# A tuned attention-plus-FFN kernel: broadcasting the reciprocal denominators in 16 reads with the head outermost in DRAM, and an instruction order that counts the issue time of transfers

## The chip, the cores and the metric

One core of one Trainium2 chip runs the whole kernel. The metric is the device time of one execution in microseconds (us). Executions of one kernel mostly agree within 0.5%. In what follows PE is TensorE (the matmuls), ACT is ScalarE, DVE is VectorE, POOL is GpSimd, and "the queue" is SyncE's, which issues every transfer.

The instructions of every engine are laid out in advance: the program holds a small scheduler that plans each operation with a counted duration and then emits one fixed list per engine. So a count in that plan that is wrong does not slow anything by itself; it puts instructions into an order that does not fit the chip.

## The reference, cut to what matters

Shapes: S = 2048 tokens, D = 1024, 32 heads of 32, F = 3584, bf16.

```python
xn = layernorm(x)
qkv = (xn @ wqkv) ...                                  # 32 heads of 32
pq, pk = phi(q), phi(k)                                # phi = elu + 1 + 1e-6
kv  = einsum("bhsd,bhse->bhde", pk, v);  z = sum_s pk
num = einsum("bhqd,bhde->bhqe", pq, kv)
den = einsum("bhqd,bhd->bhq", pq, z) + 1e-6            # one number per head and token
s = (num / den) @ wo
ffn = (silu(xn @ w_gate) * (xn @ w_up)) @ w_down
out = x + s * silu(ffn)
```

The kernel computes 1/den on a few partitions ("rows" below: one row per head), writes it to DRAM, and reads it back broadcast, each head's row to the 32 partitions that hold this head's 32 features. It then multiplies phi(q) by it before the projection.

## The kernel before: the parts that matter

The plan: an operation with a semaphore is a transfer. `free[e]` is when its queue can issue the next, `o.done` when it has landed.

```python
o.start = s
if o.sem is not None:
    free[e] = s + 0.08
    dma_free = max(s, dma_free) + o.nbytes / 310e3
    o.done = max(s + o.nbytes / 190e3, dma_free) + 1.2
else:
    ...
    free[e] = s + o.busy
    o.done = s + o.busy + o.lat
```

The denominators: for each half of the heads eight writes of 8 KB after the reciprocals, then `normalise`, which fills one tile of rows `RB` (128 partitions x 1024 elements, 256 KB) with four reads, scales it on ACT, and multiplies on DVE. It runs eight times, so there are 16 tiles, 64 reads, 32 scalings and 32 multiplies.

```python
for p in range(2):
    for q in range(4):
        t0 = (q % 2) * 256
        dma([rb], [named("rscr", p, q, s)], r_scr[p, q // 2, 16 * s:16 * s + 16, t0:t0 + 256],
            ...,  dsem("rs%d%d%d" % (p, q, s)), 8 * KB, asap=True)

def normalise(p, j, half):
    for g2 in range(2):
        RB = tmp(F2)
        rba = lambda RB=RB: vap(RB).rearrange("p (g t) -> p g t", t=512)
        for hl in range(4):
            rows = r_scr[p, j].rearrange("(g h) t -> h g t", h=4)[hl, 4 * half + 2 * g2:4 * half + 2 * g2 + 2]
            dma([...], [named("rb", RB.id, hl)], lambda ...: rba()[32 * hl:32 * hl + 32, :, :],
                rows.partition_broadcast(32), lambda ...: dsem("rr%d_%d" % (RB.slot, hl)), 64 * KB, asap=True, hold=[RB])
        for gl in range(2):
            ...
            act([z_r] + [named("rb", RB.id, hl) for hl in range(4)], [RB], zr, zr, ACT.Identity, 512, "sb", scale=zc[:, g:g + 1])
            tt([sr, RB], [sr], src.bitcast(FP16), src, zr, ALU.mult, 512, True, NE[half])     # NE = ("dve", "dve")
    ... # the product goes to q_scratch in DRAM
```

At the end the queue of transfers waits once on every semaphore that was used:

```python
for s in semn.values():
    if id(s) in PL.count:
        prog["sp"].append(("w", s, PL.count[id(s)]))
```

## Time and profile before

| what, kernel before | value | where it is from |
|---|---|---|
| time, median of 4 runs | 770.14 us (767.01 to 770.58) | timed runs |
| profiled execution | span 764.9 us, mean granted clock of TensorE 0.983 | the page |
| reads of rows | 64 of 64 KB, 2.1 us from issue to landing | the page's transfer issues |
| ACT's wait on them | 14.6 us | the waits |
| PE's waits, 150 to 260 us | 25.0 us | sum of the waits' rows |
| time in which the trace has the clock at half | 28.1 us | the trace's clock records |

### The profile page before, as it was taken

Reading aid. Unit: us, or ns where it says so; the run is one execution under the profiler, and the core shown is the slowest. Engines: PE = TensorE matmul, PEld = TensorE weight load, DVE = VectorE, ACT = ScalarE, POOL = GpSimd, SP = SyncE. Lnnn points to the kernel's source line nnn. Section 1 sums busy time; section 2 is a strip of 40 time slices with the busy share of each in tenths; the row PEclk is TensorE's granted clock in tenths of the full one; section 3 lists DMA queues with packets and bytes.
Section 4 is the critical chain, followed back from the end, with each engine's and each line's share of the span. In section 5 each row is a group of like instructions: output and inputs, shape, how many; then the busy total and the mean of one; then the engine's idle time right before and its main releaser. Section 6 shows DMA issues by size and latency. Waiting matters only on the chain.

```text
span 764.9 us, 11503 instructions
## 1 busy us (share of the span) xinstructions
PE 719.4 (94%) x4091; PEld 389.4 (51%) x4121; DVE 575.1 (75%) x1109; ACT 358.8 (47%) x677; POOL 257.8 (34%) x230
## 2 busy tenths in 40 slices
PE   8999998986969699999999999999999999999996
PEld 3444454442425366666666666665554444444442
DVE  6999766987999988888878888879997752433423
ACT  3577554866738354555555545544565111111111
POOL 2011100031592746678665687903460000000000
PEclk9999999998979899999999999999999999999999
DMA  9243314233465274313333314235599282926421
GB/s 309 76 111 70 81 26 156 71 108 114 135 181 186 87 243 129 101 56 91 102 97 104 95 52 139 69 107 180 163 359 298 78 254 83 260 91 199 131 78 40
DMA packets 142698, 101.56 MB, mean 133 GB/s; under 512 B 19504, under 2 KB 137520, under 8 KB 142640
## 3 DMA queue, kind: packets, MB, share of 16 engines
q1 hardware_dynamic: 142640, 100.82, 43.9%
q8 instruction: 32, 0.52, 0.3%
q14 instruction: 26, 0.21, 0.1%
HBM read 68.16 MB, written 29.49 MB: 128 GB/s over the span
## 4 chain that ended last, share of the span: by engine, by line
PE 77%; DVE 13%; DMA 4%; SPq 2%; issue 2%; ACT 1%; DVEq 0%; ACTq 0%
PE ps L416 77%; DVE SB L474 9%; SPq L486 2%; DMA SB<-q_scratch 1%; DMA SB<-in_A_x_dram 1%; DVE ps L474 1%; DVE SB L1032 1%; ACT SB L466 1%; DMA SB<-in_B_w_up_dram 1%; DMA SB<-r_scratch 1%; DVE SB L1030 0%; DVE stats L990 0%; DVE stats L991 0%; ACT ps L466 0%; DVE SB L1282 0%
## 5 line engine op out<-in xcount | busy, mean ns | idle before, releaser
L416 PE MATMUL ps<-SB 128*128 128x512 f16 (+3 forms) x3970 | 709.7, 339 | 34.6 <-DVE SB L474 16.4
L416 PEld LDWEIGHTS ps<-SB 128*128 128x128 f16 (+1 forms) x4000 | 383.7, 98 | 358.9 <-DVE SB L474 25.6
L474 POOL TENSOR_TENSOR SB<-SB 128x1024 f16<-128x1024 bf16 (+3 forms) x196 | 244.1, 1276 | 250.8 <-DMA SB<-in_B_w_up_dram 187.1
L466 ACT ACTIVATE SB<-ps 128x256 f32<-128x256 f32 (+4 forms) x397 | 214.4, 558 | 209.0 <-PE ps L416 195.3
L474 DVE TENSOR_TENSOR SB<-SB 128x512 f16<-128x512 f16 (+10 forms) x314 | 205.0, 687 | 71.9 <-DMA out_dram<-SB 21.0
L474 DVE TENSOR_TENSOR SB<-ps,SB 128x512 f16<-128x512 f32 (+2 forms) x318 | 182.7, 592 | 49.8 <-PE ps L416 45.3
L474 DVE TENSOR_TENSOR ps<-ps,SB 128x512 f32<-128x512 f32 (+1 forms) x238 | 123.0, 531 | 40.3 <-PE ps L416 34.6
L466 ACT ACTIVATE ps<-ps 128x512 f32<-128x512 f32 (+1 forms) x166 | 82.0, 495 | 124.4 <-PE ps L416 115.5
L466 ACT ACTIVATE SB<-SB 128x512 f16<-128x512 f32 x68 | 42.0, 619 | 48.3 <-DVE SB L474 47.4
L1032 DVE SCALAR_TENSOR_TENSOR SB<-ps,SB 128x512 bf16<-128x512 f32 x49 | 32.7, 680 | 0.3
L994 POOL TENSOR_TENSOR rstd<-veps,neg_half 128x1 f32<-128x1 f32 x16 | 11.1, 699 | 64.1 <-DVE veps L993 58.0
L1030 DVE TENSOR_SCALAR SB<-SB 128x512 f16<-128x512 f16 x64 | 18.7, 299 | 15.9 <-ACT SB L466 15.7
L466 ACT ACTIVATE SB<-SB,zc 128x512 bf16<-128x512 bf16 x32 | 22.1, 720 | 16.6 <-DMA SB<-r_scratch 14.6
L466 ACT ACTIVATE SB<-SB,nmr,rstd 128x1024 f16<-128x1024 bf16 x12 | 14.8, 1232 | 0.9 <-DVE nmr L996 0.7
L990 DVE BATCH_NORM_STATS2 stats<-SB 128x6 f32<-128x512 bf16 x16 | 10.9, 682 | 4.5 <-DMA SB<-in_A_x_dram 4.5
L1032 DVE SCALAR_TENSOR_TENSOR SB<-SB 128x512 bf16<-128x512 f32 x15 | 10.9, 727 | 0.1
L991 DVE BATCH_NORM_STATS2 stats<-SB 128x6 f32<-128x512 bf16 x16 | 10.9, 680 | 0.0
L416 PE MATMUL ps<-SB,ident 128*128 128x512 f16 x17 | 5.7, 502 | 1.4 <-POOL ident L497 1.4
L445 PE MATMUL ps<-ident,SB 128*128 128x128 f16 x40 | 3.1, 220 | 2.6 <-DVE SB L1000 1.6
L445 PEld LDWEIGHTS ps<-ident,SB 128*128 128x128 f16 x40 | 2.3, 98 | 4.4 <-DVE SB L1000 2.6
L1282 DVE RECIPROCAL SB<-SB 128x64 f32<-128x64 f32 x8 | 4.3, 539 | 0.0
L416 PEld LDWEIGHTS ps<-SB,ident 128*128 128x128 f16 x17 | 2.0, 124 | 4.2 <-issue 2.2
(28 smaller groups left out, 23.1 us busy)
## 6 DMA issues: line engine op xcount, KB each, us to landing
h_scratch<-SB SPq DMA_DIRECT2D x112, 128.0 KB, 1.7
SB<-h_scratch SPq DMA_DIRECT2D x16, 896.0 KB, 6.3
SB<-in_A_x_dram SPq DMA_DIRECT2D x32, 256.0 KB, 2.9
SB<-in_B_w_gate_dram SPq DMA_DIRECT2D x14, 512.0 KB, 4.0
SB<-in_B_w_up_dram SPq DMA_DIRECT2D x14, 512.0 KB, 5.2
SB<-in_A_wqkv_dram SPq DMA_DIRECT2D x12, 512.0 KB, 7.2
SB<-in_B_w_down_dram SPq DMA_DIRECT2D x3, 1792.0 KB, 9.2
SB<-r_scratch SPq DMA_DIRECT2D x64, 64.0 KB, 2.1
```

The lines of the kernel that those rows point to most:

```text
L416: last = h.matmul(o() if callable(o) else o, l() if callable(l) else l, r() if callable(r) else r, start=st, stop=sp, skip_group_check=True)
L445: last = h.transpose(o(), i(), ident[:, :])
L466: return op("act", reads, writes, lambda h: h.activation(ev(o), ev(i), func, **kw), n / 1200.0 + (0.055 if src == "ps" else 0.095) + (0.09 ...
L474: f = lambda h: h.tensor_tensor(ev(o), ev(a), ev(b), alu)
L486: f = lambda h: h.dma_start(ev(o), ev(i))
L990: dve([xr] + ([named("ve", 0)] if q == 1 else []), [sA], lambda h: h.bn_stats(stats[:, j, 0, :], xa[:, 0:512]), 512)
L991: dve([xr] + ([named("ve", 0)] if q == 1 else []), [sB], lambda h: h.bn_stats(stats[:, j, 1, :], xa[:, 512:1024]), 512)
L994: pool([ver, nh_r], [rsr], lambda h: h.tensor_tensor(rstd[:, j, :], veps[:, j, :], neg_half[:, :], ALU.pow), 0.56)
L1030: dve([e], [e], lambda h: h.tensor_scalar(vap(e, FP16), vap(e, FP16), 1.0, EPS_PHI, ALU.min, ALU.add), 512, 3.84, urgent=PU).port = True
L1032: dve(reads + [e], [out_r], lambda h: h.scalar_tensor_tensor(out_ap, ev(src), 0.0, vap(e, FP16), ALU.max, ALU.add), 512, urgent=PU)
L1282: dve([ea], [ra], lambda h, q=q: h.reciprocal(vap(ra, F32)[:, q * 64:q * 64 + 64], vap(ea, F32)[:, q * 64:q * 64 + 64]), 400)
```

## The change

The intent is to take 48 issues off the queue of transfers (64 reads become 16), and to tell the plan what an issue really costs. To let one read cover four heads, the scratch tensor puts the head (0 to 3 in its group) outermost.

```diff
-                free[e] = s + 0.08
+                free[e] = s + o.busy
-        r_scr = nc.dram_tensor("r_scratch", [2, 2, 32, 512], BF16)
+        r_scr = nc.dram_tensor("r_scratch", [2, 2, 4, 8, 512], BF16)
-        for k in range(F2.n):
-            for hl in range(4):
-                dsem("rr%d_%d" % (k, hl))
-            return op("sp", reads, writes, f, 0.08, sem=s, nbytes=nbytes, **kw)
+            return op("sp", reads, writes, f, 1.25 if tr else 0.45, sem=s, nbytes=nbytes, **kw)
-                    Zh[:, g, 16 + 4 * (g % 4):20 + 4 * (g % 4)], hmask[:, :], ...
+                    Zh[:, g, 16 + g % 4:32:4], hmask[:, :], ...
-   (write) r_scr[p, q // 2, 16 * s:16 * s + 16, t0:t0 + 256]
+   (write) r_scr[p, q // 2, :, 4 * s:4 * s + 4, t0:t0 + 256]
-   (four reads of 64 KB, partition_broadcast(32), a semaphore each)
+                rows = r_scr[p, j, :, 4 * half + 2 * g2:4 * half + 2 * g2 + 2]
+                dma([...], [RB], partial(vap, RB),
+                    bass.AP(tensor=rows.tensor, offset=rows.offset, ap=[[4096, 4], [0, 32], [1, 1024]]), vsem(RB), 256 * KB, asap=True)
-                    act([z_r] + [named("rb", RB.id, hl) for hl in range(4)], [RB], ...
+                    act([z_r, RB], [RB], ...
```

The new source pattern has three dimensions: 4 heads, 32 copies (step 0), 1024 elements.

More of the change, by code (lines that the diff above doesn't have):

```diff
@@ L1201, in kv_end @@
                 dve([hm_r, z_r, zh_r], [named("Zh", g)], lambda h, g=g: h.tensor_scalar(
-                    Zh[:, g, 16 + 4 * (g % 4):20 + 4 * (g % 4)], hmask[:, :], zc[:, g:g + 1], None, ALU.mult), 60)
+                    Zh[:, g, 16 + g % 4:32:4], hmask[:, :], zc[:, g:g + 1], None, ALU.mult), 60)
             for c in range(2):
@@ L1287, in den_run @@
                     t0 = (q % 2) * 256
-                    dma([rb], [named("rscr", p, q, s)], r_scr[p, q // 2, 16 * s:16 * s + 16, t0:t0 + 256],
+                    dma([rb], [named("rscr", p, q, s)], r_scr[p, q // 2, :, 4 * s:4 * s + 4, t0:t0 + 256],
                         lambda p=p, q=q: vap(rb)[32 * q + 16 * p:32 * q + 16 * p + 16, 0:256],
@@ L1294, in normalise @@
                 RB = tmp(F2)
-                rba = lambda RB=RB: vap(RB).rearrange("p (g t) -> p g t", t=512)
-                for hl in range(4):
-                    rows = r_scr[p, j].rearrange("(g h) t -> h g t", h=4)[hl, 4 * half + 2 * g2:4 * half + 2 * g2 + 2]
-                    dma([named("rscr", p, 2 * j, half), named("rscr", p, 2 * j + 1, half)], [named("rb", RB.id, hl)],
-                        lambda hl=hl, rba=rba: rba()[32 * hl:32 * hl + 32, :, :], rows.partition_broadcast(32),
-                        lambda hl=hl, RB=RB: dsem("rr%d_%d" % (RB.slot, hl)), 64 * KB, asap=True, hold=[RB])
+                rows = r_scr[p, j, :, 4 * half + 2 * g2:4 * half + 2 * g2 + 2]
+                dma([named("rscr", p, 2 * j, half), named("rscr", p, 2 * j + 1, half)], [RB], partial(vap, RB),
+                    bass.AP(tensor=rows.tensor, offset=rows.offset, ap=[[4096, 4], [0, 32], [1, 1024]]), vsem(RB), 256 * KB,
+                    asap=True)
                 for gl in range(2):
@@ L1304, in normalise @@
                     zr = lambda RB=RB, gl=gl: vap(RB)[:, gl * 512:gl * 512 + 512]
-                    act([z_r] + [named("rb", RB.id, hl) for hl in range(4)], [RB], zr, zr, ACT.Identity, 512, "sb", scale=zc[:, g:g + 1])
+                    act([z_r, RB], [RB], zr, zr, ACT.Identity, 512, "sb", scale=zc[:, g:g + 1])
                     tt([sr, RB], [sr], src.bitcast(FP16), src, zr, ALU.mult, 512, True, NE[half])
```

## The prediction

> **What bounds the kernel now.** I read the page first: its slices and shares, then PE's idle time stretch by stretch, then who made PE wait there, then the chain of waits through that stretch.
>
> ```profile
> PE 719.4 (94%) x4091; PEld 389.4 (51%) x4121; DVE 575.1 (75%) x1109; ACT 358.8 (47%) x677; POOL 257.8 (34%) x230
> ```
> TensorE is busy for 719.4 of 764.9 us, so all its idle time is 45 us. Where it lies, by stretch (columns: stretch, length, then busy us and count of PE, weight loads, DVE, ACT, POOL, then granted clock, DMA share, GB/s):
>
> ```profile
> 160.00:180.00 20.00, 14.88 (x92) 6.99 (x84) 14.54 (x29) 9.32 (x19) 6.43 (x5) 1.00 0.26 74
> 180.00:200.00 20.00, 15.22 (x97) 7.36 (x98) 17.73 (x41) 15.37 (x29) 2.13 (x3) 0.83 0.50 150
> 200.00:220.00 20.00, 15.20 (x76) 7.22 (x73) 19.13 (x26) 10.32 (x19) 19.55 (x14) 0.83 0.53 150
> 220.00:240.00 20.00, 16.41 (x97) 9.89 (x97) 18.62 (x35) 12.07 (x24) 13.32 (x11) 0.91 0.39 129
> 240.00:260.00 20.00, 13.19 (x77) 7.73 (x75) 19.41 (x29) 8.62 (x17) 12.14 (x8) 0.85 0.52 173
> 260.00:290.00 30.00, 29.91 (x190) 18.50 (x189) 24.60 (x46) 15.55 (x31) 15.32 (x13) 0.98 0.60 187
> 290.00:425.00 135.00, 135.00 (x872) 84.91 (x871) 111.31 (x201) 68.92 (x142) 90.43 (x70) 1.00 0.31 93
> ```
> From 260 us on PE is full, so whatever PE gains before 260 us should reach the end undiminished. Between 160 and 260 us PE is busy 74.9 of 100 us, and the clock falls to 0.83 to 0.91 in four of the five rows: 20 x (0.17 + 0.17 + 0.09 + 0.15) = 11.6 us of clock on top of 25.1 us of idling. That is the stage in which the denominators are written, read back 64 times and applied, so the change acts where the losses are. What PE waits for there, and what ACT waits for:
>
> ```profile
> PE ps L416 <- DVE SB L474: 15.2, 6, 6.8
> PE ps L416 <- ACT ps L466: 4.8, 4, 2.0
> PE ps L416 <- ACT SB L466: 2.4, 1, 2.4
> ...
> ACT SB L466 <- DMA SB<-r_scratch: 14.6, 11, 2.7
> ```
> ACT stands 14.6 us for the broadcast rows, and because it works in order the PSUM copies behind such a wait come late: 4.8 + 2.4 = 7.2 us of PE's waits are on ACT. The larger part, 15.2 us, is on DVE. The queue of transfers in the first burst:
>
> ```profile
> 166.31 3.57 SPq L486 DMA_DIRECT2D r_scratch<-SB  x8
> 170.00 9.66 SPq L486 DMA_DIRECT2D SB<-r_scratch  x20
> 185.82 0.34 SPq L486 DMA_DIRECT2D q_scratch<-SB  x1
> 186.21 5.96 SPq L486 DMA_DIRECT2D SB<-r_scratch  x12
> ```
> One issue takes 9.66 / 20 = 0.48 us of the queue, where the kernel's own ordering counted 0.08. So the fourth tile of rows, the 16th issue, was planned about 16 x 0.4 + 8 x 0.4 = 9.6 us too early. The chain of waits goes through just these issues: SP 15.1% and the r_scratch transfers 5.0% of the 97 us from 165 to 262, that is 14.6 and 4.9 us.
>
> **What the Trainium skill says.** (1) "DMA: Bandwidth & Descriptors", section "Rules for kernel authors": coalesce many small transfers; under 64 KB they are mostly overhead. The trace agrees: 64 KB of rows land in 2.0 us, 256 KB of A_x in 2.9 us.
> (2) The same page, section "Why a DMA increments its semaphore by 16 and not by 1": a transfer runs on the largest k up to 16 that divides the slowest dimension of both access patterns. The old read has 32 rows on both sides, so k = 16. The new source is [4 heads][32 copies][1024 elements] against 128 partitions: k = 4. No row of this trace has a source like that, so it is untested here.
> (3) "GPSIMD Engine Reference", section "Specifications": GpSimd's SBUF interfaces are shared with VectorE, with contention when a DVE instruction has two SBUF inputs. The trace agrees: the 128x512 multiply that applies the rows takes 417 ns (x6, 236 to 247 us, POOL idle), 1347 ns (x6, 207 to 222 us) and 2201 ns (x4, 247 to 257 us), the last two beside a stream of POOL instructions.
> (4) "TensorE: Matmul & The Clock Gate", "What's actually happening": after an idle window the clock halves. It agrees: around 188 to 193 us 512-column matmuls average 559 ns, against 339 ns for the main group over the whole span.
>
> **The change part by part.**
> Issues: 48 fewer reads, 48 x 0.48 = 23 us less of the queue. Only the part in the chain counts, at most the 14.6 us above, and its 8 writes (3.6 us) stay: 11 us at most.
> Landing of a tile of rows: before, four issues plus 2.0 us, and the next tile 1.9 us later; the four came at about 173.4, 175.4, 177.4, 179.3 us (ACT's starts). With k = 16, 256 KB land like an A_x tile: one issue at 170.0, landing at 172.9, the others 0.5 to 0.7 us apart, the fourth at 175, 4 us earlier. With k = 4 each of four engines carries 32 packets of 2 KB. The trace's 2 KB packets take 84 ns (median), so 32 x 0.084 = 2.7 us per tile: first at 170.0 + 0.4 + 2.7 + about 1.8 = 174.9, then every 2.7 us, the fourth at 183.0 us, 3.7 us later than now. The bytes (4 MB) are the same; packets fall from 4096 to 2048.
> Queue order: plain transfers now count as 0.45, transposes as 1.25 (the trace: 0.43 to 0.48 and 1.25), so ACT and DVE are ordered to need the rows nearer to when they come. It errs the other way where k = 4, since it counts 0.85 us per tile and not 2.7. All queues are rearranged, also where nothing was wrong; I put that scatter at some 5 us either way, by judgement.
> Weight loads: the load of the next gate tile at 193.7 us follows the second q_scratch store in its buffer. Where the multiplies finish earlier, POOL's stream of 33 us from 200.3 us starts earlier too, out of its idle time before.
> The end: the queue finishes by waiting once on every semaphore, two to an instruction, 61 ns apart in the records, from 760.1 to 764.4 us, beginning right after the last store is issued. 36 semaphores of the old reads go, about one comes: 17 x 0.061 = 1.1 us less. This one is nearly sure.
> Zh with a stride of 4 in its columns, and the 8 KB writes with 4 x 4 rows: the same number of tiny operations, nothing that shows.
>
> Sum: of the 7.2 us of PE's waits on ACT I expect about 2.5 back with k = 4, and 4.5 with k = 16; of DVE's 15.2 us, 0 to 3; the clock gives 0.5 to 1.5; the end 1.1. That is about 4.5 us with k = 4 and 9 us with k = 16. I hold k = 4 for likely, at 0.7: 0.7 x 4.5 + 0.3 x 9 = 5.9 us. 770.27 - 5.9 = 764.3; I write 764.0.
>
> **The rivals.**
> The narrow transfer takes the place of the queue: engines 0 to 3 become the bound, 16 x 2.7 = 43 us of work, spread over 170 to 240 us, and large loads queue behind them. For it: the source's outer 4. Against it: only if the rows are what DVE and PE wait for. It would make 766 to 775.
> DVE is the bound anyway: it is busy 89.4 of the 100 us, 14 of them in multiplies slowed by POOL (22 at 1059 ns in 200 to 260 us against 417: 22 x 0.64 = 14 us). Rows that all land at 208 to 225 us meet POOL's stream at its densest; those of 230 to 247 us had it to themselves. Then the gain is the tail alone, about 768.
> The order comes right: ACT no longer stands, the long pauses of 2.4 to 6.8 us vanish and with them the half clock. Up to 25.1 + 11.6 us are there to win; half of it gives 752.
>
> **Range and chances.** From the full-recovery rival to the narrow-transfer one: 753 to 771. Faster by over 2% needs 15.4 us, most of PE's idling of that stage: 0.10. Slower by over 2% needs damage in stages where PE is full: 0.02. Within 2%: 0.88.
>
> **What would show it.** Right: 16 reads of 256 KB, about 7.5 us of issue in all; the semaphore sweep shorter by 1 us; ACT's wait on r_scratch below 14.6 us but not gone; 75 to 80 us of PE in the same 100; PE full afterwards. The median landing tells k: about 3 us for 16 engines, 5 us or more for 4. Wrong: PE idle in a stage that was full before (the new order did harm), multiplies still 1 to 2 us beside POOL with PE's DVE waits at 15 us or more (no gain but the tail), or the same stage at full clock with PE above 85 (far more gain than I give).

## The result

The changed kernel takes 777.76 us (median of 4, 776.7 to 778.8) beside 770.14 us: ratio 1.0108, 95% interval 1.0078 to 1.0138. Ratios here and below are the mean time of one kernel's runs over that of the other's of the same rounds, so not quite the ratio of the medians quoted. The change costs 1.1%, about 8 us, where the prediction had a gain of 6 us, and the result lies outside its range of 753 to 771.

The page's line of busy time, kernel after:

```profile
PE 724.2 (93%) x4121; PEld 388.2 (50%) x4121; DVE 572.3 (74%) x1109; ACT 358.8 (46%) x677; POOL 258.1 (33%) x230
```

PE's totals of the two kernels can't be compared: the trace of the kernel before lacks 30 of 4121 matmul records (x4091 in the prediction's first line), nearly all before 160 us and after 580 us. In the stage of the change, between the 870th and the 1400th weight load, the records are there (535 and 532 matmuls): PE is busy 92.6 us before and 94.4 after, and idle 25.1 and 34.4 us, while the clock is at half for 23.9 and 34.1 us. So 9.3 of the 11.1 us lost there are idling, and 1.8 us can be the clock. One more caution: the profiled execution of the kernel before took 766.6 us, 3.5 us less than the median of its timed runs, and that of the kernel after 776.7, 1.1 us less. The spans of the traces differ by 10.1 us, the medians by 7.6, and every comparison below with the trace of the kernel before has this offset in it. The same stretches as in the prediction (stretch, length, busy us and count of PE, weight loads, DVE, ACT, POOL, then granted clock, DMA share, GB/s), kernel after:

```profile
160.00:180.00 20.00, 15.09 (x81) 7.31 (x79) 14.36 (x31) 9.67 (x19) 9.30 (x8) 0.95 0.18 58
180.00:200.00 20.00, 13.54 (x56) 5.94 (x57) 14.69 (x34) 12.10 (x23) 0.00 (x0) 0.63 0.51 162
200.00:220.00 20.00, 14.52 (x109) 7.87 (x108) 17.31 (x28) 11.23 (x20) 16.79 (x12) 0.97 0.32 87
220.00:240.00 20.00, 11.39 (x52) 6.00 (x51) 18.44 (x22) 7.43 (x14) 15.77 (x13) 0.69 0.38 141
240.00:260.00 20.00, 15.23 (x91) 7.81 (x90) 14.54 (x32) 11.14 (x22) 0.78 (x1) 1.00 0.52 162
260.00:290.00 30.00, 25.82 (x157) 15.12 (x156) 25.20 (x44) 14.59 (x30) 17.21 (x13) 0.94 0.39 127
290.00:425.00 135.00, 134.97 (x870) 84.52 (x868) 111.22 (x200) 69.14 (x143) 93.57 (x72) 1.00 0.36 109
```

Between 160 and 290 us PE is now busy 95.6 us (15.09 + 13.54 + 14.52 + 11.39 + 15.23 + 25.82) where it was 104.8 us, and in two of these stretches the clock is at 0.63 and 0.69. The stage of poor filling now lasts until about 290 us and not 260. After 290 us PE is full, as before.

Counting the weight loads of PE in both traces says how much is lost by when. The same load, numbered from the start, begins in the kernel after later by:

| load number (its start before, us) | 870th (160.4) | 1000th (197.8) | 1200th (238.3) | 1400th (278.1) | 3000th (529.4) | 3400th (602.1) | 4100th (753.2) |
|---|---|---|---|---|---|---|---|
| after, later by us | -0.4 | +1.4 | +8.4 | +10.7 | +8.4 | +11.5 | +11.5 |

10.7 us of it have come by the 1400th load, between 160 and 290 us. Later some 2 us come back, and 3 are lost again between the 3000th and the 3400th load; the tail of the program gives 1.4 us back, hence 10.1 us.

What the engines wait for in that stage. Kernel after, PE's and ACT's waits from 150 to 260 us (engine and line, what ended the wait; us in total, times, longest):

```profile
PE ps L413 <- DVE SB L471: 22.3, 7, 8.5
PE ps L413 <- ACT ps L463: 4.1, 3, 2.4
PE ps L413 <- ACT SB L463: 2.4, 2, 2.1
...
ACT SB L463 <- DMA SB<-r_scratch: 32.4, 12, 4.7
```

ACT's wait on the rows went from 14.6 to 32.4 us, PE's on DVE from 15.2 to 22.3 us. PE's waits on ACT stay where they were: 7.2 us before and, counted to 290 us, 7.2 us after (4.8 + 2.4). The link between the rows and PE is DVE's wait on ACT. DVE's waits before, 150 to 290 us:

```profile
DVE SB L1030 <- ACT SB L466: 6.2, 4, 4.8
...
DVE SB L474 <- ACT SB L466: 1.2, 2, 0.6
```

and after:

```profile
DVE SB L1027 <- ACT SB L463: 10.0, 7, 2.9
DVE SB L471 <- ACT SB L463: 9.9, 6, 4.5
```

L1030 and L1027 are the same line of the two files, a step of phi that takes an exponential from ACT; L474 and L471 are the multiply-and-add helper. So DVE's wait on ACT went from 7.8 us (0.4 us of it in a line left out above) to 19.9 us: ACT stands in its fixed order for a tile of rows. The multiplies that apply the rows, which did not wait for ACT before, wait 6.2 us for it now, and the exponentials behind such a wait come late too.

Why do the rows come late? The queue in the first burst, kernel after:

```profile
164.55 5.22 SPq L483 DMA_DIRECT2D r_scratch<-SB  x8
169.89 7.77 SPq L483 DMA_DIRECT2D SB<-r_scratch  x6
188.29 0.33 SPq L483 DMA_DIRECT2D q_scratch<-SB  x1
```

The issues themselves are no longer the matter: the first four tiles are issued between 169.89 and 172.4 us. But the chain of waits (start us, us, what) shows what took their place. Before, the fourth tile's last read and what followed:

```profile
176.88 0.43 SPq L486
177.35 1.98 DMA SB<-r_scratch
179.38 0.60 issue
179.99 0.59 ACT SB L466
```

After, the same tile:

```profile
171.67 12.09 DMA SB<-r_scratch
183.81 0.10 issue
183.93 0.49 issue
184.41 2.32 ACT SB L463 x4
```

Issued 5.7 us earlier than before, the fourth tile lands 4.4 us later (183.76 against 179.33). The trace's semaphore records say why. A transfer's semaphore rises to 16 in steps, the last one when all has landed. A read before takes 16 steps; a new read takes 5: one at the issue, by the queue, and 4 as its parts land. The first six new reads, each from its own records:

| tile | 1 | 2 | 3 | 4 | 5 | 6 |
|---|---|---|---|---|---|---|
| issued, us | 169.89 | 170.49 | 171.11 | 171.67 | 172.54 | 174.88 |
| landed after, us | 5.98 | 8.13 | 10.09 | 12.09 | 13.79 | 14.01 |
| landed, us | 175.9 | 178.6 | 181.2 | 183.8 | 186.3 | 188.9 |

One tile every 2.6 to 2.7 us, as 32 packets of 2 KB at 84 ns (the trace's median) on each of four engines would have it. The fifth and sixth issue also held the queue for 2.3 and 2.8 us each. Before, the last reads of the four tiles landed such that ACT started on them at 173.5, 175.4, 177.5 and 179.4 us.

### The profile page after: what moved, and what is told of

The parts are those of the page before. It is cut to its first block, busy times and chain, and to the rows that moved or that the text cites. A ratio compares the mean times of both kernels' runs of the same rounds, so it can differ in the third digit from the quotient of the medians.

```text
span 775.0 us, 11443 instructions
## 1 busy us (share of the span) xinstructions
PE 724.2 (93%) x4121; PEld 388.2 (50%) x4121; DVE 572.3 (74%) x1109; ACT 358.8 (46%) x677; POOL 258.1 (33%) x230
## 4 chain that ended last, share of the span: by engine, by line
PE 77%; DVE 12%; DMA 7%; ACT 2%; SPq 1%; issue 1%; ACTq 0%; DVEq 0%
PE ps L413 77%; DVE SB L471 8%; DMA SB<-r_scratch 4%; ACT SB L463 2%; SPq L483 1%; DVE ps L471 1%; DMA SB<-in_A_x_dram 1%; DMA SB<-q_scratch 1%; DVE SB L1029 1%; DMA SB<-in_B_w_up_dram 1%; DVE stats L987 0%; DVE SB L1027 0%; DVE stats L988 0%; ACT ps L463 0%; DVE SB L1194 0%
## 5 line engine op out<-in xcount | busy, mean ns | idle before, releaser
L471 POOL TENSOR_TENSOR SB<-SB 128x1024 f16<-128x1024 bf16 (+3 forms) x196 | 244.3, 1278 | 260.6 <-DMA SB<-in_B_w_up_dram 201.6
L471 DVE TENSOR_TENSOR SB<-SB 128x896 f16<-128x896 f16 (+10 forms) x314 | 202.4, 676 | 76.0 <-ACT SB L463 24.0
L471 DVE TENSOR_TENSOR SB<-ps,SB 128x256 f32<-128x256 f32 (+2 forms) x318 | 183.6, 593 | 56.9 <-PE ps L413 48.5
L471 DVE TENSOR_TENSOR ps<-ps,SB 128x512 f32<-128x512 f32 (+1 forms) x238 | 122.7, 531 | 39.7 <-PE ps L413 34.6
L463 ACT ACTIVATE SB<-SB 128x512 f16<-128x512 f32 (+1 forms) x68 | 42.0, 618 | 56.1 <-DVE SB L471 53.5
L463 ACT ACTIVATE SB<-SB,zc 128x512 bf16<-128x512 bf16 x32 | 22.1, 717 | 33.1 <-DMA SB<-r_scratch 32.4
L1027 DVE TENSOR_SCALAR SB<-SB 128x512 f16<-128x512 f16 x64 | 19.0, 305 | 20.8 <-ACT SB L463 20.8
```

Of the source, the lines that this page charges most:

```text
L463: return op("act", reads, writes, lambda h: h.activation(ev(o), ev(i), func, **kw), n / 1200.0 + (0.055 if src == "ps" else 0.095) + (0.09 ...
L471: f = lambda h: h.tensor_tensor(ev(o), ev(a), ev(b), alu)
L1027: dve([e], [e], lambda h: h.tensor_scalar(vap(e, FP16), vap(e, FP16), 1.0, EPS_PHI, ALU.min, ALU.add), 512, 3.84, urgent=PU).port = True
```

## The experiments

Theory N (narrow): the reads run on four engines, and the rows come late. Theory O (order): the new instruction order, made with new issue counts, is at fault. Theory C (collision): rows that come at another time only shift DVE's multiplies onto POOL's stream. Twelve kernels tell them apart. The ratio is always to the kernel before, in the same rounds. The median of the kernel before was 769.8, 769.7 and 771.5 us in the three sessions. The third session (e9 to e12) ran on another chip. So across sessions compare ratios, and small differences with care.

| run | what it is | median us | ratio, 95% interval | ACT's wait on rows, us |
|---|---|---|---|---|
| (after) | the change | 777.76 | 1.0108 [1.0078, 1.0138] | 32.4 |
| e1_order_only | before, new issue counts | 769.02 | 0.9988 [0.9959, 1.0016] | 3.8 |
| e2_transfers_only | after, old issue counts | 775.97 | 1.0075 [1.0042, 1.0108] | 32.4 |
| e4_per_head | after, four 64 KB reads per tile | 771.02 | 1.0008 [0.9980, 1.0036] | 6.9 |
| e3_wide16 | after, read on 16 engines, wrong data | 764.55 | 0.9929 [0.9899, 0.9959] | 9.5 |
| e5_k8 | after, read on 8 engines, wrong data | 769.27 | 1.0003 [0.9962, 1.0043] | 17.6 |
| e6_k2 | after, read on 2 engines, wrong data | 805.41 | 1.0454 [1.0422, 1.0486] | 63.2 |
| e9_told600 | after, read counted as 600 KB | 772.18 | 1.0016 [0.9990, 1.0041] | 18.4 |
| e7_told | after, read counted as 760 KB | 762.05 | 0.9893 [0.9867, 0.9920] | 10.5 |
| e10_told900 | after, read counted as 900 KB | 766.99 | 0.9951 [0.9928, 0.9974] | 7.3 |
| e8_pool_half1 | e1, half the multiplies on POOL | 760.24 | 0.9862 [0.9835, 0.9889] | 8.3 |
| e11_told_pool | e7 and e8's move together | 765.26 | 0.9929 [0.9907, 0.9950] | 22.5 |
| e12_short_end | e8, shorter end | 760.06 | 0.9858 [0.9834, 0.9882] | 10.4 |

### e1_order_only: the order alone

The kernel before with the two lines of issue counts alone:

```diff
-                free[e] = s + 0.08
+                free[e] = s + o.busy
-            return op("sp", reads, writes, f, 0.08, sem=s, nbytes=nbytes, **kw)
+            return op("sp", reads, writes, f, 1.25 if tr else 0.45, sem=s, nbytes=nbytes, **kw)
```

> The kernel before (64 transfers on 16 engines, old layout) with only the counted issue times changed. Theory N (the narrow read, 4 engines, is what cost the 1.1%): the new order alone does no harm, ratio to before 0.985 to 1.003, ACT's wait on the r_scratch rows 14.6 us or less. Rival O (the new order is what cost the 1.1%): ratio 1.007 to 1.015 with the reads still landing in 2 us.

Correct, 0.9988: the order alone does no harm that can be told from zero, and brings no gain. It does what it was meant to do: ACT's wait on the rows falls from 14.6 to 3.8 us, and the 1000th weight load of PE begins 7 us earlier than before (190.8 against 197.8 us). By the 1200th the order has lost that again and 2 us more (240.3 against 238.3). Stretches of e1, columns as above:

```profile
200.00:220.00 20.00, 10.85 (x49) 5.05 (x47) 16.80 (x16) 7.75 (x13) 19.92 (x14) 0.84 0.53 166
220.00:240.00 20.00, 15.99 (x87) 9.08 (x88) 17.81 (x32) 12.02 (x23) 8.22 (x9) 0.82 0.34 108
```

From 200 to 220 us POOL runs without a break (19.92 us) and DVE gets through only 16 instructions in 16.80 us. Rows that come in time meet POOL there. Theory C has part of the truth here: it says where the early win goes.

### e2_transfers_only: the transfers alone

The changed kernel with the issue counted as 0.08 again:

```diff
-            return op("sp", reads, writes, f, 1.25 if tr else 0.45, sem=s, nbytes=nbytes, **kw)
+            return op("sp", reads, writes, f, 0.08, sem=s, nbytes=nbytes, **kw)
```

> The changed kernel with the issue counted as 0.08 us again: 16 transfers on 4 engines, old way of ordering. Theory N: slow as the changed kernel or slower, ratio 1.007 to 1.02, tiles of rows landing 2 to 2.7 us apart. Rival O: back near the time before, 0.995 to 1.003.

Correct, 1.0075: the transfers alone bring the loss, in a different order, with the same 32.4 us of ACT's wait as the whole change. Theory O falls as the main cause. With e1 at 0.9988, the two parts taken alone do not quite add up to 1.0108, but the intervals are too wide to say that they interact. One difference between the orders is steady: in all 12 kernels with the new counts, the change among them, PE loses 2 to 3 us against the kernel before between the 3000th and the 3400th weight load, where the transformed q is read back, and e2 with the old order loses none (10.5 us late at both). That is a small cost of the order; why it arises there was not tested.

### e4_per_head: the new layout with the old kind of read

The head stays outermost in DRAM and the writes stay as changed, but each tile is read by four transfers of 64 KB, one head each to 32 partitions:

```diff
-   one read, ap=[[4096, 4], [0, 32], [1, 1024]], 256 KB
+                for hl in range(4):
+                    rows = r_scr[p, j, hl, 4 * half + 2 * g2:4 * half + 2 * g2 + 2].rearrange("g t -> (g t)")
+                    dma([...], [named("rb", RB.id, hl)], lambda ...: vap(RB)[32 * hl:32 * hl + 32, :],
+                        rows.partition_broadcast(32), lambda ...: dsem("rr%d_%d" % (RB.slot, hl)), 64 * KB, asap=True, hold=[RB])
```

> The new DRAM layout and the new issue times, but four reads of 64 KB a tile again, one per head, each 32 partitions of 2 KB in one piece (source outermost dimension 32, so 16 engines): a right result. Theory N: landing about 2.1 us, near e1_order_only, ratio to before 0.985 to 1.005. Rival O: 1.007 or more.

Correct, 1.0008: with 16 steps per read the loss is gone, though there are 64 issues again. Its order of instructions is e1's on every engine; it differs from e1 by the layout and the writes, which also became narrow (5 steps; the eight issues of the first burst take 5.19 us where they took 3.57 in the kernel before). That costs at most a few tenths of a per cent and is not told from zero.

### e3_wide16, e5_k8, e6_k2: the same order, another width of the read

These three change nothing but the pattern of the read. They load wrong data, since no single read can give the right data on 16 engines from this layout: the source's outermost size must be 16, and there are four heads. In their traces the order of the instructions on PE (by its weight loads), DVE, ACT and POOL, and of the transfers, is the changed kernel's.

```diff
-   ap=[[4096, 4], [0, 32], [1, 1024]]
+   ap=[[0, 128], [1, 1024]]              # e3: one row for all 128 partitions
+   ap=[[4096, 8], [0, 16], [1, 1024]]    # e5: 8 rows, from r_scr[p, 0], waits for all four writes of p
+   ap=[[4096, 2], [0, 64], [1, 1024]]    # e6: 2 rows
```

> The changed kernel, same instruction order on every engine, but each read takes one head's 1024 elements to all 128 partitions (source outermost dimension 128 and not 4): a wrong result on purpose. Theory N: 17 semaphore steps or 16 and not 5, landing about 3 us and not 6 to 14, ACT's wait on the rows falls from 32.4 us to under 10, ratio to before 0.98 to 0.995 (755 to 766 us). Rival D (DVE beside POOL sets this stage whatever the rows do): the rows come early and the time stays within 4 us of the changed kernel's 777.8. Rival O: likewise above 774.

> The changed kernel, same instruction order, each read with 8 blocks of 16 partitions (source outermost dimension 8, two blocks of it from the wrong half: a wrong result on purpose; it also waits for the writes of both halves, some 1 us). Theory N (the number of engines sets the landing): 9 semaphore steps, 16 packets of 84 ns an engine, so tiles land about 1.3 us apart, the first after about 4.5 us; time between the 16-engine run and the changed kernel, ratio to before 0.995 to 1.006. If only being below 16 counts, it is as slow as the changed kernel, 1.008 or more.

> The changed kernel, same instruction order, each read with 2 blocks of 64 partitions (source outermost dimension 2: a wrong result on purpose). Theory N: 3 semaphore steps, 64 packets of 84 ns an engine, 5.4 us a tile or somewhat less, the first after about 8 us; clearly slower than the changed kernel, ratio to before 1.02 to 1.05. Rival O (the new order): within 0.4% of the changed kernel's 1.0108.

The records show 16, 9 and 3 steps, so 16, 8 and 2 engines. This is how the Trainium skill's page "DMA: Bandwidth & Descriptors", section "Why a DMA increments its semaphore by 16 and not by 1", has it: each engine in use gives one step when its part has landed, and the issuing queue gives the missing ones at once, without waiting for data. All patterns run here agree: outermost sizes 128, 8, 4 and 2 gave 16, 9, 5 and 3 steps. The first four tiles land after these times from their issue:

| engines | 16 (e3) | 8 (e5) | 4 (after) | 2 (e6) |
|---|---|---|---|---|
| landed after, us | 3.26, 3.64, 3.81, 5.03 | 4.10, 4.82, 5.47, 6.64 | 5.98, 8.13, 10.09, 12.09 | 8.13, 12.67, 17.21, 19.61 |
| ACT's wait on rows, us | 9.5 | 17.6 | 32.4 | 63.2 |
| time at half clock, us | 19.1 | 22.7 | 39.3 | 66.6 |
| ratio | 0.9929 | 1.0003 | 1.0108 | 1.0454 |

Each halving of the width costs more, in one and the same order. That settles theory N: in this order the width of the read makes the loss. How few different rows a read takes from DRAM is no rival: e3 reads one row, e6 two, the change four. For e6 the stretch that follows the first burst, and ACT's wait, look like this:

```profile
180.00:200.00 20.00, 4.43 (x14) 1.43 (x14) 7.48 (x19) 7.75 (x14) 0.00 (x0) 0.59 0.20 79
```

```profile
ACT SB L463 <- DMA SB<-r_scratch: 63.2, 15, 6.5
```

PE is busy 4.43 of 20 us while the DMA engines have a mean share of 0.20: nearly everything stands, and most of the 16 engines as well.

e3 also estimates what the change would bring in this order if its one read ran on 16 engines: 0.9929, about 5 us, and not the 9 us that the prediction gave to 16 engines. Its stretches:

```profile
180.00:200.00 20.00, 17.05 (x122) 9.57 (x123) 18.32 (x43) 14.06 (x28) 7.44 (x5) 0.91 0.44 140
200.00:220.00 20.00, 8.99 (x42) 4.06 (x39) 19.53 (x17) 9.04 (x16) 17.92 (x12) 0.85 0.48 144
220.00:240.00 20.00, 17.69 (x102) 9.87 (x103) 18.16 (x37) 12.00 (x23) 7.54 (x8) 0.90 0.45 151
```

The pattern is e1's: full until 200 us (its 1000th weight load begins 6.8 us before that of the kernel before), then only 8.99 us of PE beside POOL's stream. DVE's instructions of that stretch in time order:

```profile
201.65 17.23 DVE L471 TENSOR_TENSOR SB<-SB 128x512 f16<-128x512 bf16 x12
```

The view merges like lines under the form of the first: of these 12 instructions, 8 are multiplies that apply the rows (1241 ns each), 3 are others on f16 (1850 ns each) and one is on f32 (2599 ns). Over the stage 160 to 280 us the 32 multiplies take 26.9 us of DVE before, 26.6 after, 28.3 in e1 and 25.7 in e3: the collision with POOL costs about the same whenever the rows come. It limits what quick rows can bring; it does not explain the loss of the change.

### e7_told, e9_told600, e10_told900: a plan that knows how slow the read is

The plan counts a 256 KB read 2.6 us to landing (256 KB / 190e3 bytes per us + 1.2) and 0.85 us for each further one (/ 310e3). The chip takes 6.0 us and then 2.6 to 2.7 us for each further one of the first burst. (The "2.1" in my expectations is the growth of the time since the issue, not the distance of the landings: a misreading.) These runs leave the data and the transfers as they are, and only count more bytes: as 760 KB, 5.3 and 2.5 us; as 600 KB, 4.4 and 2.0 us; as 900 KB, 6.1 and 3.0 us.

```diff
-   vsem(RB), 256 * KB, asap=True)
+   vsem(RB), 760 * KB, asap=True)     # e7; 600 in e9, 900 in e10
```

> The changed kernel, right result, the narrow reads kept, but the ordering counts a read as if it were 760 KB, so 2.5 us of the transfers each and 5.2 us to landing, near what the trace shows (2.1 us apart, 6.0 for the first). If the loss came of ordering ACT and DVE for rows that come later than counted, this gets much of it back: ratio to before 0.995 to 1.004 and ACT's wait on the rows under 15 us. If lateness itself costs, it stays at 1.006 or more.

> As e7_told with 600 KB counted for a read (1.9 us of the transfers, 4.4 us to landing; the trace shows 2.1 and 6.0). If e7's gain comes of counting about the truth: between the changed kernel and e7 but nearer e7, ratio to before 0.987 to 1.000. If e7 was a lucky order: anywhere up to 1.01.

> As e7_told with 900 KB counted (2.9 us of the transfers, 5.9 us to landing). Counting about the truth: near e7, ratio to before 0.986 to 0.997. A lucky order: anywhere up to 1.01.

All three are correct. e7 is at 0.9893: the same slow reads with one number of the plan put right, and it is about 16 us faster than the change (777.76 to 762.05; ratios 1.0108 to 0.9893) and faster than the kernel before. ACT's wait, e7:

```profile
ACT SB L463 <- DMA SB<-r_scratch: 10.5, 7, 3.1
```

The later stretches of e7:

```profile
240.00:260.00 20.00, 19.68 (x127) 11.98 (x126) 17.42 (x37) 13.29 (x26) 10.66 (x8) 1.00 0.40 129
260.00:290.00 30.00, 30.00 (x193) 18.62 (x192) 25.41 (x45) 15.61 (x34) 22.65 (x20) 1.00 0.62 206
```

PE is full from 240 us on, 20 us sooner than before. So slow reads need not cost time; with orders planned on slower reads, ACT stood less for them. But the new count changes more than who waits: in all three runs the queue issues four of the eight writes, then the first four reads, then the other writes, and in e7 the first read is issued at 165.04 us and not at 169.89, so its first four tiles land 4.9 us earlier than the change's. In e9 they are issued and land as in the change (5.94 to 12.04 us after the issue from 169.89 us), and ACT's wait still falls to 18.4 us and the loss to nothing that can be told from zero: there the order alone does it.

But e9 (1.0016) and e10 (0.9951) are both worse than e7, and e9 fell outside the 0.987 to 1.000 that I had expected, if narrowly. All three beat the change, which confirms the direction. 760 KB beats 900 KB by 0.6% (in another session), though 900 KB has the smaller wait on the rows (7.3 against 10.5 us). It may be that 2.5 us per tile is nearer to the measured 2.6 than 3.0 is, or that any reordering moves the time by some 0.6% either way; these runs do not tell. How much of e7's 1.1% is a better plan and how much is such chance stays open.

### e8_pool_half1, e11_told_pool: the collision with POOL

In e8 the kernel before gets e1's counts, and the second half's 16 multiplies go to POOL:

```diff
-    NE = ("dve", "dve")
+    NE = ("dve", "pool")
```

> The order-only kernel with the 16 multiplies of the second half put on GpSimd instead of DVE. Theory D (what the early rows win by 198 us is given back at 200 to 260 us where DVE's multiplies stand beside POOL's stream): DVE no longer stands in multiplies of 1 to 2 us there, PE's waits on DVE after 200 us fall from about 20 us to under 12, ratio to before 0.985 to 0.998. Rival P (POOL itself becomes late with 16 x 1.2 us more, and the next gate tiles with it): 1.0 or more.

Correct, 0.9862: faster than the kernel before by 1.4%, and than e1 by 1.3% (ratios), so this one line is worth 9 to 10 us, in which the chance of a new order may have a share. Stretches of e8:

```profile
220.00:240.00 20.00, 15.16 (x84) 7.87 (x83) 10.00 (x20) 12.96 (x24) 18.46 (x17) 0.91 0.48 153
240.00:260.00 20.00, 19.24 (x123) 11.19 (x120) 15.73 (x30) 11.16 (x24) 19.77 (x16) 1.00 0.49 158
```

DVE's load from 220 to 240 us falls to 10.00 of 20 us, and PE has 19.24 of 20 us from 240 us, where it had 14.32 in e1 (13.19 in the kernel before). PE's waits from 150 to 300 us fall to 19.2 us, from 28.3 in e1 and 25.0 in the kernel before; those on DVE after 200 us fall from 18.3 us in e1 to 6.9, as expected. The 16 multiplies cost POOL 18.9 us; those left to DVE take 675 ns each, where all 32 took 933 ns in e1. How much comes of DVE's shorter list and how much of fewer collisions was not separated.

e11 is e7 with the same line:

> e7_told with the second half's 16 multiplies on GpSimd as in e8. If the late rows and DVE beside POOL are two separate losses, the gains add in part: ratio to before 0.975 to 0.986. If they are the same waits seen twice, no better than e8's 0.986 (0.984 to 0.993).

Correct, 0.9929: worse than e8 and not better than e7 (its interval overlaps e7's). The expectation that the two gains add (0.975 to 0.986) is refuted; the other one, "the same waits seen twice" (0.984 to 0.993), had the number, but no run shows that reason. ACT's wait on the rows is back at 22.5 us, from 10.5 in e7. The multiplies' move changes the order around the reads, and the narrow reads are late for it again. I take this as the same lesson from another side: with reads of 2.6 us a tile every change of order is a new risk; what exactly put them out of step was not looked into.

### e12_short_end: the end of the program

e8, with one semaphore for the four reads of a tile, and the final waits only on the semaphores of the pool from which the output is stored:

```diff
-            for hl in range(4):
-                dsem("rr%d_%d" % (k, hl))
+            dsem("rr%d" % k)
-        for s in semn.values():
-            if id(s) in PL.count:
+        for n, s in semn.items():
+            if id(s) in PL.count and n.startswith("f2_"):
```

> e8_pool_half1 with one semaphore for the four reads of a tile, and at the end waits on the semaphores of the stores of the result alone: same order of instructions. The sweep at the end was 4.8 us before and 3.4 us in the changed kernel from the issue of the last store; it should fall to about 2 us, set by the landing of that store. Ratio to before 0.9862 - 0.0036 = 0.982 to 0.984. If the end is set by something else, 0.986 again.

Correct, 0.9858, and 0.9862 for e8 in an earlier session on another chip: no difference to be told. In the trace the end is shorter, as meant: 2.4 us from the issue of the last store to the end, where it is 5.2 us in the kernel before (5 waiting instructions; 67 before, 61 ns apart). But PE of this execution reached its last weight load at 752.7 us where e8's was at 750.7 us, which takes most of that back, though the order of instructions is the same on every engine. One profile of each cannot say whether this is chance. So the saving is shown in the trace and not in the time; the expected 0.982 to 0.984 was missed.

e8 and e12 are the best versions with right results, both about 1.4% faster than the kernel before and 2.4% faster than the change.

## Why the prediction was wrong

**What bounds the kernel.** Right: the time is set between 160 and 260 us, and what happens there reaches the end. Every kernel whose PE gained or lost there kept it, but for the 2 to 3 us that the new counts cost later (told under e2).

**Narrow or wide.** Right: four engines, given 0.7. The steps of the semaphore and the landings of e3, e5 and e6 show it, and the landing times were close: 174.9 and 183.0 us predicted for the first and fourth tile, 175.9 and 183.8 measured. The page prints no landing for these reads, so the sign I had named, a median of 5 us or more, had to be taken from the records.

**The sum, the step that failed.** It said: "of the 7.2 us of PE's waits on ACT I expect about 2.5 back with k = 4". The paragraph before it had just worked out that the fourth tile comes 3.7 us later than now, and that the plan counts 0.85 us per tile where the engines need 2.7. Later rows, under an order that expects them earlier, cannot shorten a wait on rows. I set the certain gain (issues saved) into the sum and left the cost, which I had in numbers, as a remark. Term by term, from 150 to 300 us: PE's waits on ACT, of which 2.5 us were to come back, stayed at 7.2 us. PE's waits on DVE, where I had 0 to 3 us of gain, went from 17.8 to 27.0 us, which is the whole growth of PE's waits (25.0 to 34.2). So the path was wrong too: ACT's wait on the rows went from 14.6 to 32.4 us, DVE's on ACT from 7.8 to 19.9, and the delay reached PE through DVE, not through the PSUM copies. PE was 10.7 us late by the 1400th load. The clock, for which I gave 0.5 to 1.5 us of gain, was at half for 39.3 us and not 28.1, but the added time fell on an idle PE (from 130 to 320 us it was busy for 18.9 us of the half-clock time before and 19.9 after): PE's busy time in the stage grew by 1.8 us. The error per tile adds up: 12 waits of up to 4.7 us, not one.

**Other slips in the working.** The terms for k = 4 add up to 4.1 to 8.1 us; my 4.5 took nearly all of them at the low end. The 11.6 us "of clock on top" of the idling are too many, since PE stood idle for 5.0 of the 22.9 us at half clock between 160 and 260 us. The 339 ns of point (4) are the mean of a group with four shapes; the 512-column matmul alone takes 379 ns at full clock, to set beside the 559 ns. The "45 us" of idling are somewhat too many, because of the 30 missing records.

**The count of the plan.** The prediction named it ("0.85 us per tile and not 2.7") and gave it no cost. e7, e9 and e10 show that it matters about as much as the width: the same slow reads, counted as slower, come out at 0.9893 to 1.0016 instead of 1.0108.

**The issues.** 48 issues went, but not 23 us of queue time. The issues of the reads took 28.0 us in all before and 12.6 after, not the 7.5 I had named, as two of them held the queue for 5.1 us; those of the 16 writes rose from 6.6 to 9.9 us. That leaves 12 us. The gain went back at once: the path that had run through the issues runs through the landing (12.09 us for the fourth tile).

**The rivals.** The first, "the narrow transfer takes the place of the queue", is what happened, and its 766 to 775 was too mild by 3 us (which four of the 16 engines carry the reads, the records do not show). It should have been the main line, as k = 4 had 0.7. The second, DVE bound by POOL, holds where rows are quick: e1 and e3 win 7 us by the 1000th load; by the 1200th e1 has given back all of it and e3 all but 2.1 us. So 16 engines bring 5 us (e3) and not 9. The third, that the order comes right, did not come.

**The scatter of the order.** My 5 us either way was about right: e7, e9 and e10 differ by 10 us from one count of the plan. e1 puts the new counts alone at zero within 3 us.

**The end.** 17 waiting instructions fewer, 1.4 us measured for 1.1 predicted. Right.

**The signs named.** ACT's wait was to fall below 14.6 us and rose to 32.4; PE was to be busy for 75 to 80 of the 100 us and was for 69.8. Two of the signs of being wrong came: PE idle in a stage that was full (25.82 of 30 us from 260 us), and waits on DVE above 15 us. The reason given there, "the new order did harm", is not the main one by e1 and e2.

**The chances.** "Within 2%" had 0.88 and came true; the range was too narrow at its upper end: it was built around a centre that had the wrong sign, and its 771 cut off nearly half of the 766 to 775 that its own first rival gave.

## What to carry to other kernels

Before you merge small transfers, look at the outermost dimension of both patterns: fewer issues on fewer engines can be a loss, and the time from issue to the last landing decides. Where a plan fixes the order of instructions, put the measured landing of each kind of transfer into it, and when your own working says that something comes later, carry that number into the sum. A gain that comes earlier than a neighbouring stream on another engine expects can be eaten there, so look at what the freed work will run beside (here, moving 16 multiplies to POOL was worth more than all the transfers).

## What the Trainium skill lacked or had wrong

- "DMA: Bandwidth & Descriptors", section "Rules for kernel authors": the rule to coalesce many small transfers stands without a condition, and the row "Use all 16 engines" of the same table, which names the trap of an outermost size below 16, gives no cost. Here 16 reads of 256 KB on four engines landed 6.0 to 14.0 us after their issue (first six) and on 16 engines 3.3 to 5.3 us. With the four-engine reads the kernel was 1.1% slower than with 64 reads of 64 KB (0.75% with the old issue counts, e2).
- The same page has no size for what a narrow transfer costs the queue that issues it on this chip: writes of 8 KB with k = 4 took 0.58 us to issue against 0.42 us with k = 16 (the pattern changed with k). Reads of 256 KB that followed each other closely held the queue from the fifth on with k = 4 (2.3 and 2.8 us), from the third on with k = 2 (2.7 to 6.1 us), and not at all with k = 8 (0.6 us each).
- No page that I found has the cost of waiting on many semaphores at the end of a program: 61 ns for an instruction that waits for two, 67 such instructions before the change and 50 after.
